# Two weight chunks a step for the quarters, late routing one slot sooner, one-hots ahead of a split, matmuls on zeros at the start, last product in tile order

## The chip, the cores and the metric

The kernel runs on one core of a Trainium2 chip. The metric is the device time of one execution, in microseconds, from all inputs in HBM to all outputs in HBM. The engines are named as in the profile: PE (TensorE), PEld (its weight loads), DVE (VectorE), ACT (ScalarE), POOL (GpSimd) and SP (SyncE, which here issues DMAs).

## What is computed

Three layers in a row, all in fp32: sigmoid attention, a mixture of eight experts with one expert for each token, and a dense layer with a squared ReLU. Cut to what matters (q and k are drawn 4.906 times larger than the 0.1 of the first line):

```
B, H, S, D = 4, 12, 448, 64          # q, k, v: randn * 0.1
scores = q @ k.T / sqrt(D) - log(S)
attn = 1 / (1 + exp(-scores)) @ v    # 1792 tokens x 768
# experts: w_gate (768, 8), w1 (8, 768, 1024), w2 (8, 1024, 768)
logits = x @ w_gate; e = argmax(logits)
gate = exp(logits - max)[e] / (sum(exp(logits - max)) + 1e-9)
x = gate * (relu(x @ w1[e]) @ w2[e])
# dense: w_in (768, 2048), w_out (2048, 768)
h = relu(x @ w_in)
out = (h * h) @ w_out
```

## The kernel before

**Precision.** A product that has to be as exact as fp32 is made of three products of a faster type (fp32r): each operand is split into a high part (ACT copies it into fp32r) and a low part (DVE subtracts), and PE forms high by high, low by high and high by low. The split of a weight chunk (128 x 1536) is `split_w`: wh by ACT (L473), wl by DVE (L474).

**Attention (5.8 to about 180 us).** 24 units, each a pair of heads of one batch. `score` writes score tiles to two PSUM banks (L372, L374), ACT takes the sigmoid (L376), `av` multiplies by v (L382, L385). Unit 0 uses plain fp32 scores, straight from the loaded q and k; the later units use the split form. PE has nothing to do before the first load has come. Finished units are transposed (xn, L421 to L423) and written to x_d in HBM; gate logits come from xT, and `token_logits` copies them into lg (L415). `head` (L190 to L196) makes the one-hots of the experts and their running sum cum. Its first call covers the first three batches, so that the largest expert's tokens can begin early; its second call, at the end of the attention, covers the fourth.

**Expert slots (about 180 to 504 us).** The tokens are sorted by expert into slots of 128; 15 slots are always run, s = 0 to 14. Each has eight steps, c = 0 to 7, one weight chunk each: four of `up` (products ph, L680 to L682), four of `down` (py). Behind each half of `up` ACT takes the ReLU (hr, L722), PE transposes it (L705), ACT and DVE split it (hh L706, hl L707). Behind each step `next_chunk` splits the chunk for the next slot and SP issues the load for the slot behind that. In c = 5 the next slot's rows are transposed, in c = 6 and 7 `fin` copies y out of PSUM (L739) and writes it.

**Routing.** Slots 0 and 1 (FS = 2) hold the early expert. In slot 0 `opening` counts the tokens of all experts on PE (`counts`, L200 to L202, from cum and the one-hots), computes the slots and places on DVE (`slots`, L244 to L257; `late_places`; `spots`, which fills A, L212). In slot 1, c = 0, `pick_rows` turns these into row numbers, by which POOL gathers. In slot 1, c = 6, `late_routing` computes the later slots' rows and gates: 18 small DVE instructions (L815 to L833), one exponential on ACT, three products on POOL (Bg, L837), and SP loads three row starts into registers.

**Quarters.** Up to four remainders of at most 32 rows, NQ = 4, run beside slots 3 to 12. Every two steps there is one event of ten: e = 0 transposes the 32 rows into PSUM tile qa and ACT copies them to qxT; e = 1 to 4 multiply by one `up` chunk each (L785, four matmuls side by side in column groups of 32); e = 5 transposes the hidden rows; e = 6 to 9 take the `down` chunks (L805), and the last copies the result to yq on ACT and writes it. A chunk (128 x 1536) is loaded by `q_load` three chunks ahead (QB = 3 buffers).

**Dense layer (504 to 953 us).** For each of two blocks (4 and 3 token tiles on either half): first layer (pp, L1031 to L1033), then seven products (pq, L1134 to L1136) that make up a Strassen-like scheme; `evac` adds them up on DVE (ob, L1095), and `scatter` (L1001, POOL) writes rows to the output by token number. The last block's last product ends the kernel: its three scatters are issued behind everything else.

**What sets the order.** The order of the program text is the order on each engine; buffers and semaphores do the rest. `order.close()` ends that ahead of the last three scatters.

Of the kernel before, what the change touches and what calls it, by code (L numbers as in the profile page):

```python
# [10 lines left out]
F32 = mybir.dt.float32  # L11
# [11 lines left out]
DM = H * D  # L23
E = 8
# [21 lines left out]
QB = 3  # L46
CH = 1536
# [17 lines left out]
def moe_kernel(ctx: ExitStack, tc: tile.TileContext, qk, v, wg, wm, w2, out):  # L65
# [87 lines left out]
    lg = rt([CP, NR, E], "lg")  # L153
# [3 lines left out]
    eq, z, ez = (rt([CP, NR, E], n) for n in ("eq", "z", "ez"))  # L157
    posA, t30 = rt([CP, E, NR], "posA"), rt([128, E], "t30")
    posi, sli = (rt([CP, NR], n, I32) for n in ("posi", "sli"))
    plf = rt([CP, NR], "plf")  # L160
    A, Bs, Bt = rt([CP, NR, 128], "A", F16), rt([CP, NR, LC], "Bs", F16), rt([CP, NR, LC], "Bt", F16)
# [162 lines left out]
    with ExitStack() as actx:  # L324
# [107 lines left out]

        prev = None
# [129 lines left out]
        token_logits()  # L563
        split_first(2)
        head(FR, NR)
# [89 lines left out]
    with ExitStack() as mctx:  # L655
        w2p = mctx.enter_context(tc.tile_pool(name="w2p", bufs=1, side="right", reuse_waits="tile"))
        mp = mctx.enter_context(tc.tile_pool(name="mp", bufs=2, reuse_waits="tile"))
        ps_x = mctx.enter_context(tc.tile_pool(name="ps_x", bufs=1, space=PS, reuse_waits="tile"))
        ps_h = mctx.enter_context(tc.tile_pool(name="ps_h", bufs=1, space=PS, reuse_waits="tile"))
# [96 lines left out]
        def q_load(n):  # L756
# [5 lines left out]
            qr[n] = mp.tile([128, CH], F32, tag="qraw", name=f"qraw{n}", bufs=QB)  # L762
# [3 lines left out]

        def q_event(k):
            q, e = divmod(k, 10)
            if e == 0:
                qt[0] = ps_q.tile([128, 512], F32, tag="q", name=f"qa_{q}")  # L770
                for j in range(KD):
                    nc.tensor.transpose(qt[0][:, QM * j:QM * j + QM], qx[q][:QM, j * 128:(j + 1) * 128], ident[:QM, :QM])
                qt[1] = mp.tile([128, 256], F32, tag="qT", name=f"qxT_{q}", bufs=1)[:, :KD * QM].rearrange("p (a b) -> p a b", a=KD)
                nc.scalar.activation(qt[1].rearrange("p a b -> p (a b)"), qt[0][:, :KD * QM], AF.Copy)
                if q + 1 < NQ:
                    q_gather(q + 1)
            elif e < 5:
                n = 8 * q + e - 1
                c = QORD[n % 8]
                w = qr.pop(n)  # L780
                o = KD * QM + (c // 2) * 128
                for i in range(3):
                    kk = 3 * (c % 2) + i
                    for j in range(4):
# [6 lines left out]
            elif e == 5:  # L791
                qt[0] = ps_q.tile([128, 512], F32, tag="q", name=f"qb_{q}")
                qt[3] = mp.tile([128, 256], F32, tag="qT", name=f"qhT_{q}", bufs=1).rearrange("p (a b) -> p a b", a=2)
                for i in range(2):
                    nc.tensor.transpose(qt[0][:, i * 128:i * 128 + 128], qt[2][:, i, :], ident)
# [407 lines left out]
```

## Time and profile before

| | us |
|---|---|
| median of 3 runs (lowest, highest) | 963.2 (962.22, 964.21) |
| the profiled execution | 963.18 |
| its span, first to last instruction | 961.7 |
| PE busy | 935.9 (97% of the span) |
| DVE busy | 631.2 (66%) |
| ACT busy | 551.4 (57%) |
| POOL busy | 78.8 (8%) |
| mean granted clock of PE | 0.993 |

How to read it: the span has no long holes on PE. A saving on another engine counts only where PE waits for that engine at that moment; a saving on PE counts everywhere but in a stretch whose end another engine sets. The profile shows one execution; its times are microseconds from the start of the span.

### The profile page before, as it was taken

What the parts mean: (1) busy time and instruction counts of PE and PEld (TensorE: products, weight loads), DVE (VectorE), ACT (ScalarE), POOL (GpSimd) and SP (SyncE); (2) the same over time, 40 slices, a digit from 0 to 9 for tenths busy, and PEclk for the clock granted to TensorE, in tenths of its full rate; (3) what the DMA queues carried; (4) which work ended last, traced back from release to release, by engine and by line L of the source; (5) the groups of instructions that cost most, each with busy time, mean ns of one, the idle gap of its engine ahead of it and who ended that gap; (6) DMA issues with size and microseconds to landing.
All of it is one profiled execution on the core that took longest, in us unless ns stands there. A gap on an engine that the chain in (4) does not pass through costs nothing. (4 is left out here: it accounts for less than half of the span.)

```text
span 961.7 us, 15015 instructions
## 1 busy us (share of the span) xinstructions
PE 935.9 (97%) x5869; PEld 784.7 (82%) x5869; DVE 631.2 (66%) x706; ACT 551.4 (57%) x667; POOL 78.8 (8%) x106
## 2 busy tenths in 40 slices
PE   7999999898999999999998999999999999999996
PEld 3555555487888888888987888889999999999996
DVE  2788866589877776777865676747857521228762
ACT  5767665557777767767753454454534444446550
POOL 1000001024311010100000000010000210000002
PEclk9999999999999999999999999999999999999998
DMA  8798967481487869694447455363244532223312
GB/s 290 255 368 300 357 217 267 164 312 38 170 283 300 326 242 368 225 397 148 162 174 261 183 196 231 132 247 101 97 132 148 169 112 66 66 66 114 117 33 98
DMA packets 52512, 190.63 MB, mean 198 GB/s; under 512 B 8082, under 2 KB 18962, under 8 KB 50386
## 3 DMA queue, kind: packets, MB, share of 16 engines
q1 hardware_dynamic: 34290, 152.77, 45.1%
q0 software_dynamic: 6928, 31.08, 8.4%
q10 hardware_dynamic: 11216, 5.75, 2.1%
q8 instruction: 48, 0.79, 0.3%
q14 instruction: 30, 0.25, 0.1%
HBM read 203.33 MB, written 36.98 MB: 250 GB/s over the span
## 5 line engine op out<-in xcount | busy, mean ns | idle before, releaser
L474 DVE TENSOR_TENSOR wl<-raw,wh 128x1536 fp32r<-128x1536 f32 x110 | 192.6, 1761 | 63.8 <-ACT wh L473 62.0
L473 ACT ACTIVATE wh<-raw 128x1536 fp32r<-128x1536 f32 x110 | 162.9, 1483 | 2.7 <-PE ph L682 0.6
L376 ACT ACTIVATE a<-sc,bias_s 128x896 f32<-128x896 f32 x96 | 82.6, 910 | 56.1 <-PE sc L372 56.0
L1037 ACT ACTIVATE r<-pp 128x512 f32<-128x512 f32 (+1 forms) x64 | 34.8, 544 | 107.4 <-PE pp L1033 107.4
L1134 PE MATMUL pq<-wrh,sh 128*128 128x384 f32 x264 | 89.0, 337 | 0.3 <-DVE ob L1095 0.3
L1135 PE MATMUL pq<-wrl,sh 128*128 128x384 f32 x264 | 88.6, 336 | 0.0
L1136 PE MATMUL pq<-wrh,sl 128*128 128x384 f32 x264 | 88.6, 336 | 0.0
L680 PE MATMUL py<-wh,hh 128*128 128x384 f32 x240 | 84.6, 353 | 0.0
L682 PE MATMUL py<-wh,hl 128*128 128x384 f32 x240 | 81.0, 338 | 2.7 <-DVE hl L707 2.7
L681 PE MATMUL py<-wl,hh 128*128 128x384 f32 x240 | 80.8, 337 | 0.0
L680 PE MATMUL ph<-wh,xh 128*128 128x512 f32 x180 | 75.7, 421 | 1.6 <-ACT xn L422 1.6
L474 DVE TENSOR_TENSOR wrl<-raw,wrh 128x1536 fp32r<-128x1536 f32 x30 | 52.6, 1757 | 36.0 <-ACT wrh L473 36.0
L473 ACT ACTIVATE wrh<-raw 128x1536 fp32r<-128x1536 f32 x30 | 44.4, 1482 | 48.0 <-PE pq L1136 43.1
L682 PE MATMUL ph<-wh,xl 128*128 128x512 f32 x180 | 71.6, 398 | 0.0
L681 PE MATMUL ph<-wl,xh 128*128 128x512 f32 x180 | 71.6, 398 | 0.0
L1045 DVE TENSOR_TENSOR h<-h,h 128x512 f32<-128x512 f32 (+1 forms) x16 | 10.0, 624 | 85.9 <-ACT h L1040 85.9
L1058 DVE TENSOR_TENSOR sl<-h,sh 128x1024 fp32r<-128x1024 f32 (+1 forms) x56 | 59.8, 1085 | 8.7 <-ACT sh L1057 8.6
L382 PE MATMUL po<-a,qkv 128*64 128x448 f32 x288 | 59.6, 548 | 0.0
L1057 ACT ACTIVATE sh<-h 128x1024 fp32r<-128x1024 f32 (+1 forms) x56 | 51.5, 943 | 13.5 <-PE pq L1135 8.0
L1134 PEld LDWEIGHTS pq<-wrh,sh 128*128 128x128 f32 x264 | 49.6, 188 | 0.6 <-issue 0.6
L1135 PEld LDWEIGHTS pq<-wrl,sh 128*128 128x128 f32 x264 | 49.6, 188 | 0.0
L1136 PEld LDWEIGHTS pq<-wrh,sl 128*128 128x128 f32 x264 | 49.6, 188 | 0.0
(289 smaller groups left out, 2088.5 us busy)
## 6 DMA issues: line engine op xcount, KB each, us to landing
raw<-in_wm SPq DMA_DIRECT2D x110, 768.0 KB
qraw<-in_wm SPq DMA_DIRECT2D x32, 768.0 KB
raw<-t_d SPq DMA_DIRECT2D x28, 768.0 KB
cs<-in_w SPq DMA_DIRECT2D x9, 1536.0 KB
raw<-w_d SPq DMA_DIRECT2D x16, 768.0 KB
qkv<-in_qk SPq DMA_DIRECT2D x23, 480.0 KB
whc<-in_w SPq DMA_DIRECT2D x7, 1536.0 KB
t_d<-wlc POOLq DMA_DIRECT2D x7, 1536.0 KB, 7.6
```

Of the source, the lines that this page charges most:

```text
L376: nc.scalar.activation(a[:, :n], ps[:, :n, :S], AF.Sigmoid, bias=bias_s, scale=1.0 / math.sqrt(D))
L382: nc.tensor.matmul(po[64 * h:64 * h + 64, :S], vr[:, 128 * c + 64 * h:128 * c + 64 * h + 64], a[:, h], start=(c == 0), stop=False, skip_gr ...
L473: nc.scalar.activation(h, src, AF.Copy)
L474: nc.vector.tensor_tensor(l, src, f32(h), op=ALU.subtract)
L680: nc.tensor.matmul(ps, lh, rh, start=first, stop=False)
L681: nc.tensor.matmul(ps, lh, rl, start=False, stop=False)
L682: nc.tensor.matmul(ps, ll, rh, start=False, stop=last)
L1057: nc.scalar.activation(sh[:, :2 * N], src, AF.Copy)
L1058: V.tensor_tensor(sl[:, :2 * N], src, f32(sh[:, :2 * N]), op=ALU.subtract)
L1134: nc.tensor.matmul(po[p][:, :DH], lh, wc[:, w0:w0 + DH], start=(q == 0 and kk == 0 and o in (0, 2, 5)), stop=False, **fl)
L1135: nc.tensor.matmul(po[p][:, :DH], lh, wcl[:, w0:w0 + DH], start=False, stop=False, **fl)
L1136: nc.tensor.matmul(po[p][:, :DH], ll, wc[:, w0:w0 + DH], start=False, stop=(q == 3 and kk == 1), **fl)
```

## The change

1. Ahead of the first scores DVE clears a 128 x 448 tile, and PE multiplies it by itself three times, 400 columns, plain fp32, into a bank that nobody reads.
2. The second call of `head` stands ahead of `split_first(2)`.
3. The pool of ph's banks is opened ahead of the pool of the transposes' banks, so each takes other banks of PSUM.
4. `late_routing` is called in slot 1 at c = 0, behind the row numbers and the gathers, no longer at c = 6.
5. lg, z, ez, posA and A lie in one tile `big`, which later serves as a fourth buffer for quarter chunks (each n with n % 4 == 3); chunks are loaded four ahead (QL = 4).
6. A quarter has five events, one every four steps (c = 2 and c = 6 of slots 3 to 12): two `up` chunks, two `up` chunks, the transposes of the hidden rows, two `down` chunks, two `down` chunks. Behind the last of them come yq and, in the same event, the next quarter's transposes (`q_rows`).
7. The last product of the last block runs with the tile as the outer loop and the four parts as the inner one; both remaining splits stand in front of it.

```
+        rest_t = xp.tile([128, S], F32, name="rest_t")
+        nc.vector.memset(rest_t, 0.0)
+        pw = ps_e.tile([128, 512], F32, tag="lgT", name="pw")
+        for i in range(3):
+            nc.tensor.matmul(pw[:, :400], rest_t[:, :128], rest_t[:, :400], start=True, stop=True, skip_group_check=True)
...
         token_logits()
+        head(FR, NR)
         split_first(2)
-        head(FR, NR)
         split_first(3)
...
+        ps_h = mctx.enter_context(tc.tile_pool(name="ps_h", bufs=1, space=PS, reuse_waits="tile"))
         ps_x = mctx.enter_context(tc.tile_pool(name="ps_x", bufs=1, space=PS, reuse_waits="tile"))
-        ps_h = mctx.enter_context(tc.tile_pool(name="ps_h", bufs=1, space=PS, reuse_waits="tile"))
...
+    big = rq.tile([128, CH], F32, tag="big", name="big")
+    lg, z, ez = (big[:CP, 1024 + 128 * i:1152 + 128 * i].rearrange("p (t e) -> p t e", e=E) for i in range(3))
...
+            if n % 4 == 3:
+                qr[n] = rq.tile([128, CH], F32, tag="big", name=f"qraw{n}")
+            else:
+                qr[n] = mp.tile([128, CH], F32, tag="qraw", name=f"qraw{n}", bufs=QB)
...
         def q_event(k):
+            q, e = divmod(k, 5)
+            if e == 2:
+                q_hidden(q)
+                return
+            for r in ((0, 1), (2, 3), (), (4, 5), (6, 7))[e]:
+                (q_up if e < 2 else q_down)(q, r)
+            if e == 4:
+                q_out(q)
                 if q + 1 < NQ:
+                    q_rows(q + 1)
...
+        q_due = {8 * (FS + 1) + 2 + 4 * k: k for k in range(5 * NQ)}
...
                         xg[k] = gather(k)
+                    late_routing()
...
-                if s == 1 and c == 6:
-                    late_routing()
...
+            if lastb and o == len(PRODS) - 1:
+                split_s(4 * o + 2)
+                split_s(4 * o + 3)
+                for p in range(P):
+                    for q in range(4):
+                        product(o, q, p, used[0] + q // 2)
+                break
```

`q_up`, `q_hidden`, `q_down`, `q_rows` and `q_out` are the bodies of the old events, and `product` is the body of the old loop over the tiles.

At three places the order on an engine is shown. DVE at the end of the attention, before (lg: the gate logits; ohz and cum: the one-hots and their running sum; wl: the low part of a weight chunk):

```order
L415 COPY lg<-lgT_1677 112x32
L474 TENSOR_TENSOR wl_1772<-raw_1466,wh_1771 128x1536
L190 TENSOR_REDUCE m<-lg 112x4
L191 TENSOR_TENSOR eq<-lg,m 112x32
L192 TENSOR_TENSOR z<-lg,m 112x32
L193 TENSOR_TENSOR eq<-eq,rev 112x32
L194 TENSOR_REDUCE me<-eq 112x4
L195 TENSOR_TENSOR ohz<-eq,me 112x4x8
L196 SCALAR_TENSOR_TENSOR cum<-seg,ohz 112x136
L474 TENSOR_TENSOR wl_1772<-raw_1466,wh_1771 128x1536
```

The same place on DVE now (lg and z lie in big):

```order
L418 COPY big<-lgT_1679 112x32
L193 TENSOR_REDUCE m<-big 112x4
L194 TENSOR_TENSOR eq<-big,m 112x32
L195 TENSOR_TENSOR big<-big,m 112x32
L196 TENSOR_TENSOR eq<-eq,rev 112x32
L197 TENSOR_REDUCE me<-eq 112x4
L198 TENSOR_TENSOR ohz<-eq,me 112x4x8
L199 SCALAR_TENSOR_TENSOR cum<-seg,ohz 112x136
L482 TENSOR_TENSOR wl_1774<-raw_1468,wh_1773 128x1536 x2
```

The seven instructions of the one-hots moved from between the two splits to ahead of both.

DVE at the start of slot 1, before (idx, tok: the row numbers picked; hl: the low part of the hidden tile):

```order
L273 CAST idx<-r_1872 128x24
L274 TENSOR_SCALAR tok<-r_1872 128x24
L474 TENSOR_TENSOR wl_1473<-raw_1466,wh_1471 128x1536
L474 TENSOR_TENSOR wl_1474<-raw_1466,wh_1472 128x1536
L707 TENSOR_TENSOR hl_2095<-pht_0_2153,hh_2094 128x512
```

And now, the end of the same stretch (the late routing's first 11 instructions stand ahead of these, behind idx and tok):

```order
L852 TENSOR_TENSOR r_128<-r_128,srowT 128x20
L853 CAST gp<-gr 112x16
L854 TENSOR_SCALAR beyond<-r_128,sx 128x20
L855 TENSOR_TENSOR r_128<-r_128,beyond 128x20
L856 TENSOR_SCALAR ctl<-r_128 128x20
L857 TENSOR_TENSOR gr<-gr,gp 112x16
L858 CAST gp<-gr 112x16
L482 TENSOR_TENSOR wl_1475<-raw_1468,wh_1473 128x1536
L482 TENSOR_TENSOR wl_1476<-raw_1468,wh_1474 128x1536
L715 TENSOR_TENSOR hl_2097<-pht_0_2205,hh_2096 128x512
```

The late routing now stands between the row numbers and the first two splits of slot 1.

PE in slot 5 at c = 2, the end of the first quarter, before (qb: the quarter's result):

```order
L705 MATMUL pht_0_3115<-ident,hr_0_3103 128x128 x4
L680 MATMUL ph_1_3108<-wh_1771,xh_2955 128x512
L681 MATMUL ph_1_3108<-wl_1772,xh_2955 128x512
L682 MATMUL ph_1_3108<-wh_1771,xl_2956 128x512
L805 MATMUL qb_2880<-qraw_2938,qhT_2881 32x96 x16
L680 MATMUL ph_1_3108<-wh_1771,xh_2955 128x512
```

And now (qa: the next quarter's transposes):

```order
L713 MATMUL pht_0_3101<-ident,hr_0_3089 128x128 x4
L688 MATMUL ph_1_3094<-wh_1773,xh_2941 128x512
L689 MATMUL ph_1_3094<-wl_1774,xh_2941 128x512
L690 MATMUL ph_1_3094<-wh_1773,xl_2942 128x512
L817 MATMUL qb_2884<-qraw_2769,qhT_2885 32x96 x16
L817 MATMUL qb_2884<-qraw_2785,qhT_2885 32x96 x16
L781 MATMUL qa_3156<-ident,qx_2610 128x32 x6
L688 MATMUL ph_1_3094<-wh_1773,xh_2941 128x512
```

The last two chunks stand in a row, and the next quarter's transposes, which stood two steps later, stand right behind them; they write the bank that yq is copied from.

## Rows read from the trace of the kernel before

**Rows 1.** Waits of PE: line, waited for, us in total, times, longest.

```profile
PE r L200 <- DVE cum L196: 2.9, 1, 2.9
PE py L682 <- DVE hl L707: 2.7, 1, 2.7
PE ph L680 <- ACT xn L422: 1.6, 1, 1.6
```

**Rows 2.** Timeline of the opening: start, length, engine, line, [idle before <- releaser].

```profile
5.84 4.51 PE L372 MATMUL sc<-qkv 64*128 64x448 f32 x12 [5.84 <-DMA qkv<-in_qk]
...
11.46 0.47 PE L372 MATMUL sc<-qkh 64*128 64x448 f32 x2
...
12.87 2.48 PE L382 MATMUL po<-a,qkv 128*64 128x448 f32 x12
...
9.25 2.75 ACT L376 ACTIVATE a<-sc,bias_s 128x896 f32<-128x896 f32 x3 [0.46 <-PE sc L372]
```

**Rows 3.** Windows: us, PE busy, other engines, granted clock, DMA share, GB/s.

```profile
5.84:10.35 4.51, 4.51 (x13) 1.74 (x13) 2.58 (x4) 2.01 (x2) 0.00 (x0) 1.00 1.04 392
...
187.49:190.91 3.42, 3.42 (x11) 0.52 0.01 2
...
236.25:254.00 17.75, 17.75 (x123) 1.00 0.59 195
```

**Rows 4.** Timeline of slot 0, DVE and ACT.

```profile
183.88 1.76 DVE L474 TENSOR_TENSOR wl<-raw,wh 128x1536 fp32r<-128x1536 f32 x1 [3.23 <-ACT wh L473]
...
186.77 0.44 DVE L196 TENSOR_TENSOR_SCAN cum<-seg,ohz 112x136 bf16<-112x136 bf16 x1
...
191.33 0.60 ACT L722 ACTIVATE hr<-ph 128x512 f32<-128x512 f32 x1 [0.24 <-PE ph L682]
...
195.27 0.68 DVE L707 TENSOR_TENSOR hl<-pht,hh 128x512 fp32r<-128x512 f32 x1
```

**Rows 5.** Timeline of slot 1 and the start of slot 2, DVE.

```profile
209.16 1.76 DVE L474 TENSOR_TENSOR wl<-raw,wh 128x1536 fp32r<-128x1536 f32 x1 [0.84 <-ACT wh L473]
212.30 1.76 DVE L474 TENSOR_TENSOR wl<-raw,wh 128x1536 fp32r<-128x1536 f32 x1 [1.39 <-ACT wh L473]
...
226.00 0.16 DVE L815 TENSOR_TENSOR sa<-sa 128x8 f32<-128x8 f32 x1
...
229.85 5.74 DVE L474 TENSOR_TENSOR wl<-raw,wh 128x1536 fp32r<-128x1536 f32 x3
```

**Rows 6.** Timeline of POOL, the late routing's products.

```profile
227.38 0.84 POOL L837 TENSOR_TENSOR Bg<-Bs,gp 112x384 bf16<-112x384 f16 x1 [15.63 <-DVE gp L824]
...
230.00 2.31 POOL L837 TENSOR_TENSOR Bg<-Bs,gp 112x384 bf16<-112x384 f16 x1 [0.62 <-DVE gp L833]
```

**Rows 7.** Timeline of a quarter's event on PE, and one wh on ACT.

```profile
253.32 0.39 PE L682 MATMUL ph<-wh,xl 128*128 128x512 f32 x1
253.64 0.86 PE L785 MATMUL qa<-qraw,qxT 128*32 128x128 f32 x24
254.43 0.50 PE L680 MATMUL ph<-wh,xh 128*128 128x512 f32 x1
254.77 0.40 PE L681 MATMUL ph<-wl,xh 128*128 128x512 f32 x1
255.00 0.40 PE L682 MATMUL ph<-wh,xl 128*128 128x512 f32 x1
...
265.76 1.48 ACT L473 ACTIVATE wh<-raw 128x1536 fp32r<-128x1536 f32 x1
```

**Rows 8.** Groups of the page: line engine op, count, busy, mean ns, idle before.

```profile
L1058 DVE TENSOR_TENSOR sl<-h,sh 128x1024 fp32r<-128x1024 f32 (+1 forms) x56 | 59.8, 1085 | 8.7 <-ACT sh L1057 8.6
```

**Rows 9.** Timeline of the end, DVE and POOL.

```profile
952.26 0.97 POOL L1001 DMA_INDIRECT out<-ob,idx  x1 [3.66 <-DVE ob L1095]
...
953.02 0.56 DVE L1095 TENSOR_TENSOR ob<-pq,ob 128x384 f32<-128x384 f32 x1 [0.49 <-PE pq L1136]
...
954.82 0.97 POOL L1001 DMA_INDIRECT out<-ob,idx  x1 [0.30 <-issue]
```

More of the change, by code (lines that the diff above doesn't have):

```diff
@@ new lines, in q_rows @@
+        def q_rows(q):
+            qt[0] = ps_q.tile([128, 512], F32, tag="q", name=f"qa_{q}")
+            for j in range(KD):
+                nc.tensor.transpose(qt[0][:, QM * j:QM * j + QM], qx[q][:QM, j * 128:(j + 1) * 128], ident[:QM, :QM])
+            qt[1] = mp.tile([128, 256], F32, tag="qT", name=f"qxT_{q}", bufs=1)[:, :KD * QM].rearrange("p (a b) -> p a b", a=KD)
+            nc.scalar.activation(qt[1].rearrange("p a b -> p (a b)"), qt[0][:, :KD * QM], AF.Copy)
+            if q + 1 < NQ:
+                q_gather(q + 1)
@@ new lines, in q_up @@
+        def q_up(q, r):
+            n = 8 * q + r
+            c = QORD[n % 8]
+            w = qr.pop(n)
+            o = KD * QM + (c // 2) * 128
+            for i in range(3):
+                kk = 3 * (c % 2) + i
+                for j in range(4):
+                    nc.tensor.matmul(qt[0][QM * j:QM * j + QM, o:o + 128], qt[1][:, kk, :], w[:, i * 512 + 128 * j:i * 512 + 128 * j + 128],
+                                     start=(kk == 0), stop=(kk == KD - 1), skip_group_check=True, tile_position=(0, QM * j))
+            if r == 3:
+                qt[2] = mp.tile([128, 256], F32, tag="qh", name=f"qh_{q}", bufs=1).rearrange("p (a b) -> p a b", a=2)
+                nc.scalar.activation(qt[2].rearrange("p a b -> p (a b)"), qt[0][:, KD * QM:KD * QM + 256], AF.Relu)
+            q_load(n + QL)
@@ new lines, in q_hidden, with q_down @@
+        def q_hidden(q):
+            qt[0] = ps_q.tile([128, 512], F32, tag="q", name=f"qb_{q}")
+            qt[3] = mp.tile([128, 256], F32, tag="qT", name=f"qhT_{q}", bufs=1).rearrange("p (a b) -> p a b", a=2)
+            for i in range(2):
+                nc.tensor.transpose(qt[0][:, i * 128:i * 128 + 128], qt[2][:, i, :], ident)
+            nc.scalar.activation(qt[3].rearrange("p a b -> p (a b)"), qt[0][:, :256], AF.Copy)
+        def q_down(q, r):
+            n = 8 * q + r
+            c = QORD[n % 8]
+            fg, dh = (c - 4) // 2, c % 2
+            w = qr.pop(n)
+            o = 256 + 96 * dh
+            for f in range(4):
+                for j in range(4):
+                    nc.tensor.matmul(qt[0][QM * j:QM * j + QM, o:o + 96], qt[3][:, fg, QM * f:QM * f + QM], w[:, f * 384 + 96 * j:f * 384 + 96 * j + 96],
+                                     start=(fg == 0 and f == 0), stop=(fg == 1 and f == 3), skip_group_check=True, tile_position=(0, QM * j))
+            q_load(n + QL)
@@ L943, in moe_kernel @@
                     nc.gpsimd.dma_start(out=yq_d[:, :, DM:DM + 1].rearrange("q t a -> t q a"), in_=tok[:QM, NSLOT:].bitcast(F32).unsqueeze(2))
[L944 removed]
+                    for n in range(QL):
                         q_load(n)
@@ L1127, in moe_kernel @@
                 for p in range(P):
[L1128 to L1138 removed]
+                    product(o, q, p, used[0])
+                sp.pop(g)
                 adds(o, q)
```

97 lines of the change are left out of this document (29 added, 68 removed).

## Prediction

> **What bounds the kernel now.** I began with the page: PE is busy for 935.9 of the 961.7 us of the span, so time is to be won where PE waits, where it runs at half clock, or where its records show overhead beside streaming. Next came the list of what PE waited for [rows 1]. Its largest entry, the first load, is not touched; three others lie where the change acts: 2.9 us for the running sum of the one-hots, 2.7 for the low half of a hidden tile, 1.6 for a copy out of the bank that the first MoE product takes. Together 7.2 us. Then I read four stretches in order of time: the opening [rows 2], slot 0 [rows 3, 4], slots 1 and 2 [rows 5, 6], one event of a quarter [rows 7], and at the end the last product [rows 8, 9]. The profiled run took 963.18 us and its span 961.7, so 1.5 us lie around the span; the median of the three runs is 963.2, the same within 0.02. I subtract every gain from 963.18. A difference of 0.2% (1.93 us) is about what a measurement of this kernel can tell from none.
>
> **Opening matmuls on zeros: gain 1.2 us.** The six plain fp32 score matmuls of unit 0 (12 records) take 4.51 us from 5.84; six fp32 matmuls of the same columns, paired in the same way, take 2.48 at 12.87 [rows 2]. The first ones ran at about half rate, 1.2 GHz instead of 2.4, after an engine that had done nothing. Yet the granted clock of 5.84 to 10.35 reads 1.00 [rows 3]; the record and the durations disagree, and I go by the durations. If the zeros lift the clock in time, a score tile takes 2.48/3 = 0.83, the first is there at 6.67, and then ScalarE's sigmoids are the limit, because there are two score banks: three at about 2.75/3 = 0.92 make 2.75, so the next unit's scores start at about 9.4, with the way from engine to engine about 9.8, instead of at 11.46 [rows 2]. That is 1.66 at the most. Nothing is the other end, and below that the zeros could run into the load's arrival and delay PE by a few tenths (−0.3). I take 1.2, since the clock may rise only within the first tile. PE has no other wait until slot 0 in the list [rows 1], so a shift there arrives.
>
> **Slot 0: gain 1.2 us.** The swap of the pools takes ph out of the bank that xn is copied from, and the 1.6 us wait goes; the one-hots ahead of the split take the 2.9 us wait [rows 1]. These sums don't add up, because VectorE's chain sets the end of slot 0. Before its split at 183.88 VectorE is idle for 3.23 us; then the one-hots end at 186.77 + 0.44 = 187.21, and all that follows runs almost back to back to hl at 195.27 to 195.95, which PE's first down product takes [rows 4]. The split begins at 183.88 in any case (it waits for ScalarE), the one-hots, 187.21 − (183.88 + 1.76) = 1.57 us of work, fit into the idle 3.23, and the chain behind them comes 1.57 sooner. This is the upper end. PE finishes sooner than that, so its wait moves on to hr at 191.33 and the hl behind it [rows 4]: if the clock falls in that wait as it did to 0.52 behind the present one (187.49 to 190.91 [rows 3]), 3.42 × 0.48 = 1.6 us are lost, as they are now, and the end is still VectorE's. Lower end: nothing, if the first pass over the hidden tile waits for ScalarE's own split. I take 1.2.
>
> **Late routing a slot sooner: gain 1.1 us.** Now its 18 small VectorE instructions run from 226.00 to 229.85, 3.85 us, and the three splits behind it take 5.74 [rows 5]; at their end the hidden tile's low half is late by 2.73 (2.7 in [rows 1]), and this wait goes. In slot 1 the same 3.85 us are put behind the picked rows, ahead of the splits at 209.16 and 212.30. VectorE is idle there for 0.84 and 1.39, 2.23 together [rows 5]. What doesn't fit, 3.85 − 2.23 = 1.62, makes hl, next behind the splits, late, and PE waits for it: 2.73 − 1.62 = 1.1. Bounds: 2.0, if the routing's own gaps close up; −0.8, if only part of the idle time can be used (3.5 us of stall). ScalarE's one exponential and the three products on GpSimd move along. So do SyncE's three register loads: they wait for the row starts, and the weight loads of that step are queued behind them, which are needed a slot later.
>
> The third product on GpSimd began at 230.00, under a split, and took 2.31, against 0.84 for one that didn't [rows 6]: GpSimd waited, not VectorE. The Trainium skill ("SBUF — State Buffer", section "SBUF: two separate sides") says that a VectorE operation with two SBUF inputs and a GpSimd operation that reads SBUF exclude each other, whichever begins first, for a whole instruction. By that rule the splits of slot 1 can be held up as well, by three products of 0.84, about 2.5 at the worst; part of it would still be idle time, and the time would come out near 957.4. I keep to the row, in which the split went first.
>
> **Quarters: gain 2.8 us.** At a chunk's event [rows 7] PE starts 0.09 late (253.32 + 0.23 = 253.55, start 253.64), the 24 records take 254.43 − 253.64 = 0.79 until the next matmul, and that one lasts 0.34 (to 254.77) where its follower lasts 0.23 (to 255.00): 0.20 of switching beside the body. Two chunks in a row save this once: 0.20 for each of 16 pairs, 3.2. The body may hold such a share too: its 12 fp32 matmuls (two records each) run four side by side, so three times 128 columns stream, and at 0.83 us for 448 columns [rows 2] that is 0.71 of the 0.79. I take this 0.08 along: 0.28 × 16 = 4.5. The next quarter's six transposes behind the last pair save about 0.2 at three places, 0.57. Against this: they write the bank from which yq is still to be copied, so they wait for ScalarE, and there yq stands behind wh of the same step, 1.48 us [rows 7], which can only begin when PE has ended that chunk's matmuls. A pair lasts 2 × 0.79 = 1.58, so wh is covered and the copy itself is not: below the 0.60 that the larger hr copy takes [rows 4], 0.58 with the way. At the one place of the three where the step also has a y copy ahead of wh, another 0.5 by the same row: 0.58 + 1.1 + 0.58 = 2.26. Sum 4.5 + 0.57 − 2.26 = 2.8. Ends: 0.4 (0.20 a pair, the waits half as long again) and 4.0 (the waits half as long).
>
> The Trainium skill ("TensorEngine Tiling (Array Packing)", section "Key Properties") says that a change of the tiling mode drains TensorE. The 0.09 ahead of the group agrees. By this rule the transposes behind a pair are one more change, and keeping them there saves about 0.3 less over the three places; the time would be 956.7.
>
> **Last product tile by tile: gain 0.5 us.** The three last scatters go one behind the other from 952.26, and the last starts at 954.82, though its sum on VectorE is over at 953.02 + 0.56 = 953.58 [rows 9]. With the tiles in turn the first two scatters are long gone, and the last one starts when its sum is there: at most 1.24 sooner. Other end: the two splits now stand together in front, and the first tile reaches the fourth part sooner; a split is 1.085 us on VectorE [rows 8], so −1.1 if the second is late by a whole one. I take 0.5.
>
> The packing of scratch into one tile costs nothing: the same instructions on other addresses, and the fourth buffer's first load waits for the last use of that scratch in slot 2, before the point where the loads are issued.
>
> **Sum.** 1.2 + 1.2 + 1.1 + 2.8 + 0.5 = 6.8; 963.18 − 6.8 = 956.4. All best ends together, 1.66 + 1.57 + 2.0 + 4.0 + 1.24 = 10.5, would give 952.7.
>
> **Rivals.**
> *A: ScalarE takes the quarters' gain.* If yq and the copies of the next quarter stand behind more of ScalarE's work than I counted, the pairs save 0.20 each and the waits at three places double (4.5): 3.2 + 0.57 − 4.5 = −0.7 in place of 2.8, time about 959.9. For it: at every one of these places wh waits for PE itself. Against: only three places.
> *B: the routing falls on slot 1 in full*, 3.5 us of stall against 2.73 removed (−0.8 in place of 1.1), and slot 0 gains nothing because its end waits for ScalarE: 956.4 + 1.9 + 1.2 = 959.5; with a half-clock stretch like that at 187.49 [rows 3], 1.6 more, 961.1. For it: VectorE's idle time in slot 1 is itself a wait for ScalarE's splits.
> *C: the zeros don't do what they are there for.* The granted clock at the start already reads 1.00 [rows 3], and then nothing is to be lifted: 956.4 + 1.2 = 957.6.
> *D, the other side: the second chunk of a pair is late.* Now a chunk is used every two steps; then two at once, and both come through one queue between the reloads. A chunk of 128 x 1536 fp32 numbers, 786 KB, at the 195 GB/s of 236.25 to 254.00 [rows 3] takes about 4.0 us. If at six of the pairs (two for each quarter at its start, whose loads have only eight steps' lead, three quarters) half a transfer is missing, PE waits 6 × 2.0 = 12: 968.4. It is slower than before as soon as the 16 pairs wait 6.8/16 = 0.43 us each in mean. Against: the list has no wait for a chunk of a quarter at all [rows 1], the DMA share there is 0.59 [rows 3], and a fourth buffer is added.
>
> **How the numbers follow.** Forecast 0.54, A 0.17, B 0.13, C 0.10, D 0.06. The range of 8 in 10 takes the forecast with its bounds, A, C and most of B: 952.7 to 961.0. Faster by over 0.2% is below 961.25: the forecast, C, A and B but for the part in which they coincide (some 0.09), 0.84. Within 0.2%: that part, 0.09. Slower: D and a little, 0.07.
>
> **What would show it.** Opening: the 12 records of unit 0 take about 2.5 to 3.5 us, and the next scores start near 10. Slot 0: neither the wait for cum nor that for xn is in the list; a wait for hr's transposes or for hl, at a PE end 1.2 to 1.6 us sooner, is. Slots 1 and 2: no wait for hl in slot 2, one of 1.3 to 1.7 in slot 1; B is right if it is above 2.7. Quarters: 16 pairs that each cost about 1.7 beside the matmuls around them (now 2 × 0.99: 254.77 − 253.55 less 0.23), and three waits of 0.5 to 1.2 ahead of the transposes; A is right if they come to over 4. Tail: the last scatter starts under 1 us behind the last sum. The prediction is wrong if a wait for qraw stands in the list, or if half clock spreads over the slots that now run at 1.00.

## The result and the profile after

The changed kernel takes 951.92 us (median of 4 runs, 950.93 to 953.03) against 963.71 (4 runs, 962.22 to 964.72): a ratio of 0.9879, 95% interval 0.9862 to 0.9897. It is 11.8 us faster; 6.8 were forecast, and the time lies below the range. Both kernels were profiled twice (963.18 and 964.24 us before, 953.03 and 951.19 after). Cut at the same instructions of TensorE, the two pairs show where the time went (us saved; a minus is a loss):

| stretch | forecast | first pair | second pair |
|---|---|---|---|
| opening, to the first product by v | 1.2 | 0.33 | 1.49 |
| attention's end and slot 0 | 1.2 | 2.63 | 3.21 |
| slots 1 and 2 | 1.1 | −1.24 | 0.25 |
| slots 3 to 14 (quarters) | 2.8 | 3.78 | 3.71 |
| start of the dense layer to its first pq | 0 | 4.38 | 4.04 |
| the rest of the dense layer | 0 | −0.19 | −0.12 |
| from the last product's final records to the end | 0.5 | 0.46 | 0.47 |
| sum | 6.8 | 10.15 | 13.05 |

The largest row is one that the forecast does not have. First the list of TensorE's waits in the kernel after (line, waited for, us, times, longest), to be laid beside [rows 1]:

```profile
PE py L690 <- DVE hl L715: 2.4, 1, 2.4
PE qa L781 <- ACT yq L823: 2.0, 3, 0.9
PE pht L713 <- ACT hr L730: 2.0, 1, 2.0
PE pw L440 <- DVE rest_t L437: 1.7, 1, 1.7
PE pp L1056 <- ACTq L986: 0.7, 1, 0.7
PE sc L375 <- ACT a L379: 0.5, 2, 0.4
```

All three waits of [rows 1] are gone, and waits of much the same length for hl and hr have come, the first a slot earlier than before. Seen from this list alone little was won. What else is gone is a wait that [rows 1] left out, because nothing in the change touches its place. In the list of the kernel before it stands between the 2.7 and the 1.6:

```profile
PE pp L1032 <- issue: 2.6, 1, 2.6
```

Timeline of the kernel before, behind the jump over the extra slots (the slots beyond the 15, which a branch at L961 skips; in the kernel after it is at L986):

```profile
504.36 0.47 PE L1031 MATMUL pp<-yt,wrh 128*128 128x512 f32 x1 [0.86 <-ACTq L961]
507.44 0.39 PE L1032 MATMUL pp<-yt,wrh 128*128 128x512 f32 x1 [2.61 <-issue]
```

And its window there (us, PE busy and the other engines, granted clock, DMA share, GB/s):

```profile
508.00:512.00 4.00, 4.00 (x12) 3.10 (x11) 3.93 (x3) 0.00 (x0) 0.00 (x0) 0.57 1.01 407
```

TensorE runs one product, waits 2.61 us for nothing that the list names ("issue"), and then has a mean granted clock of 0.57 over 4 us, the 1.2 GHz level for most of them. The same place after:

```profile
498.86 0.50 PE L1056 MATMUL pp<-yt,wrh 128*128 128x512 f32 x1 [0.71 <-ACTq L986]
499.19 0.40 PE L1057 MATMUL pp<-yt,wrh 128*128 128x512 f32 x1
499.43 0.40 PE L1058 MATMUL pp<-yt,wrl 128*128 128x512 f32 x1
```

No wait, and no half clock (1.00 from 498 to 502): 4.38 us.

### The profile page after: what moved, and what is told of

It is laid out like the page before. It is cut to its first block, busy times and chain, and to the rows that moved or that the text cites. A ratio compares the mean times of both kernels' runs of the same rounds, so it can differ in the third digit from the quotient of the medians.

```text
span 951.5 us, 15019 instructions
## 1 busy us (share of the span) xinstructions
PE 933.4 (98%) x5875; PEld 787.7 (83%) x5875; DVE 631.7 (66%) x707; ACT 552.3 (58%) x667; POOL 80.3 (8%) x106
```

## Experiments

Each kernel was timed beside the kernel before; since that kernel's median differs between the chips (962.5 to 964.1), kernels are compared by their ratios to it, and a difference of ratios is turned into us at 963.7. The intervals of the ratios are some ±0.002, ±2 us, so a term of 1 us is read from the traces.

### Moving the jump's target without doing anything else

```diff
+        tiny_t = xp.tile([128, 32], BF16, name="tiny_t")
+        nc.vector.memset(tiny_t, 0.0)
+        pw = ps_e.tile([128, 512], F32, tag="lgT", name="pw")
+        for i in range(8):
+            nc.tensor.matmul(pw[:32, :32], tiny_t, tiny_t, start=True, stop=True, skip_group_check=True)
         prev = None
```

> The kernel before, with eight bf16 matmuls of 32 x 32 on zeros at the very start, where TensorE waits for the first load anyway; nothing else differs. In the trace of before, TensorE runs one product behind the jump over the extra slots (504.36), waits 2.61 us with no releaser named, and then runs at a granted clock of 0.57 until about 511.5; the same stretch lasts 4.38 us less in the changed kernel. Theory P (place of the code): the wait is a fetch of TensorE's instructions, and it is there because the target of the jump lies a few instructions ahead of the end of a fetched block; eight more matmuls ahead of it move the target past that end, so the wait and the half clock go: 4.4 us less, about 959.3, with no 'issue' wait at the dense layer's start. The Trainium skill (Runtime: NRT & Kernel Launch, section Instruction fetch mechanics) says that a taken branch to a target outside the fetched blocks stalls. Rival R (an effect of the change on other engines or queues, or chance of one execution): the wait of 2.6 stays, time within 1 us of before.

Measured: 957.87 us against 963.08, ratio 0.9949 (0.9931 to 0.9967), 5 us less from eight matmuls that compute nothing. In its list of waits there is no "issue" any more, only

```profile
PE pp L1036 <- ACTq L966: 0.7, 1, 0.7
```

and the stretch from the dense layer's start to its first pq lasts 4.43 us less than in the kernel before. Theory P holds, and R falls: none of the seven changes is in this kernel. (It does clear a tile and use a bank more; the kernel with two zeros below has no such difference. Ahead of the dense layer its trace gains 0.9: 2.2 by the end of slot 0, of which 1.6 are lost in slots 1 and 2; both are taken up below.)

### Without the zeros, and with two of them

```diff
-        rest_t = xp.tile([128, S], F32, name="rest_t")
-        nc.vector.memset(rest_t, 0.0)
-        pw = ps_e.tile([128, 512], F32, tag="lgT", name="pw")
-        for i in range(3):
-            nc.tensor.matmul(pw[:, :400], rest_t[:, :128], rest_t[:, :400], start=True, stop=True, skip_group_check=True)
```

```diff
-        for i in range(3):
+        for i in range(2):
             nc.tensor.matmul(pw[:, :400], rest_t[:, :128], rest_t[:, :400], start=True, stop=True, skip_group_check=True)
```

> The changed kernel without the opening matmuls on zeros and their clearing. The opening: the trace of after has the second unit's scores only 0.34 us sooner than before, so I expect 0.3 us lost there (my prediction of 1.2 would mean 1.2). By theory P the three fp32 matmuls are also twelve TensorE instructions ahead of the jump; without them its target lies about five instructions ahead of where it was in before, so that four or so products run behind the jump, and then the wait returns, shorter: 1.5 to 2.2 us, with half clock behind it, 3 to 4 us in all, total 955 to 956. By rival R nothing returns at the dense layer's start, total near 952.3.

> The changed kernel with two instead of three matmuls on zeros (1.7 to 4.6 us instead of 1.7 to 6.1). If the clock has risen by the first scores all the same, these take 2.5 for 12 records and start at the load's arrival. If it falls back or hasn't risen in the gap, the 12 records take about 4.5 again, as without zeros. For theory P this is a third place of the jump's target, four TensorE instructions ahead of the changed kernel's and eight behind that without zeros, which ran four products before it waited 2.20: it lies at the end of a block then, and either there is no wait or one of 2.6 to 3 with no or one product ahead of it.

Measured: 956.47 (ratio 0.9928, 0.9914 to 0.9943) without them, 4.7 more than the changed kernel; 957.18 in one run with two. Timeline of TensorE without the zeros, where the dense layer starts:

```profile
498.96 0.47 PE L1051 MATMUL pp<-yt,wrh 128*128 128x512 f32 x1 [0.87 <-PEq L981]
499.27 0.40 PE L1052 MATMUL pp<-yt,wrh 128*128 128x512 f32 x1
499.50 0.40 PE L1053 MATMUL pp<-yt,wrl 128*128 128x512 f32 x1
499.73 0.40 PE L1051 MATMUL pp<-yt,wrh 128*128 128x512 f32 x1
502.33 0.43 PE L1052 MATMUL pp<-yt,wrh 128*128 128x512 f32 x1 [2.20 <-issue]
```

The same with two zeros:

```profile
501.78 0.40 PE L1056 MATMUL pp<-yt,wrh 128*128 128x512 f32 x1 [3.78 <-issue]
```

This kernel differs from the changed one by a single matmul, so no bank, no tile and no other engine is left as the cause. The instructions of TensorE can serve as a ruler. Each fp32 matmul on zeros is two records and two weight loads, and each product of the dense layer one record and one weight load. Counted in the traces up to the first product (pp), with the place of the wait:

| kernel | instructions ahead | products before the wait | wait | block landed | TensorE goes on |
|---|---|---|---|---|---|
| changed, no zeros | 7002 | 4 | 2.20 | 500.94 | 502.33 |
| before, pools swapped (below) | 7006 | 2 | 2.01 | 504.21 | 505.70 |
| before | 7008 | 1 | 2.61 | 506.06 | 507.44 |
| before, second trace | 7008 | 1 | 2.29 | 507.06 | 508.54 |
| changed, two zeros | 7010 | 0 | 3.78 | 500.34 | 501.78 |
| changed (three zeros) | 7014 | no wait | | 500.41 | |

With two instructions for each product that ran, and the weight load of the next, the wait stands behind instruction 7011 in all five traces that have it (the 3.78 includes the 0.7 to 0.9 that every kernel waits at the jump); the twelve traces without it count 7014 to 7023 ahead of the first product. That there were four products without zeros, and one in the kernel before, is due to six instructions more in the latter, all of them waits for semaphores.

The page of each trace lists TensorE's instructions as a DMA queue of their own: 16 KB a packet, one packet for some 246 of TensorE's 11806 instructions. The kernel before, and then the kernel after:

```profile
q8 instruction: 48, 0.79, 0.3%
```

```profile
q8 instruction: 47, 0.77, 0.3%
```

The five traces with the wait have 48 packets, the twelve others 47. The times of single packets (the column "block landed") show what is waited for. The jump's own record lasts 3.5 to 4.0 us in every trace and ends 1.36 to 1.39 behind the landing of a packet. The Trainium skill ("Runtime: NRT & Kernel Launch", section "Instruction fetch mechanics") says that a taken branch whose target isn't in the window of instructions already fetched waits for a fetch; the traces agree. The next packet starts only 0.7 to 1.5 behind the end of the jump; where nine instructions or fewer are left of the target's block, TensorE runs out of them and goes on 1.38 to 1.49 behind that packet's landing. Where the target lies in the block behind, 12 to 16 products run by that time, and nothing is waited for. So the wait that the list calls "issue" is one for instructions.

The zeros' own effect: opening of the kernel after, the same place in its second trace, and then the opening with two zeros.

```profile
1.73 4.37 PE L440 MATMUL pw<-rest_t 128*128 128x400 f32 x6 [1.73 <-DVE rest_t L437]
6.16 2.46 PE L375 MATMUL sc<-qkv 64*128 64x448 f32 x8
...
11.12 0.48 PE L375 MATMUL sc<-qkh 64*128 64x448 f32 x2 [0.16 <-ACT a L379]
```

```profile
5.90 1.77 PE L375 MATMUL sc<-qkv 64*128 64x448 f32 x8 [0.39 <-DMA qkv<-in_qk]
```

```profile
1.74 3.03 PE L440 MATMUL pw<-rest_t 128*128 128x400 f32 x4 [1.74 <-DVE rest_t L437]
5.76 4.87 PE L375 MATMUL sc<-qkv 64*128 64x448 f32 x12 [0.99 <-DMA qkv<-in_qk]
...
11.73 0.47 PE L375 MATMUL sc<-qkh 64*128 64x448 f32 x2
```

Two matmuls and a pause of 0.99 us leave the scores at half rate (4.87 for 12 records, 4.51 in [rows 2]). Three lift it: behind the first tile in the first trace, without a pause (8 records in 2.46), and from the first record in the second, with a pause of 0.39 (1.77). Whether the third matmul or the shorter pause does it was not separated. Rival C falls, although the granted clock reads 1.00 in all these windows, as in [rows 3]. The first product by v starts at 11.45 to 12.54 in eleven traces with three zeros and at 12.74 to 13.59 in six without or with two: about 1.2 on the mean, as forecast, and the first trace of the kernel after had the latest start of its eleven.

### Late routing: back, and in pieces

```diff
                         xg[k] = gather(k)
-                    late_routing()
...
+                if s == 1 and c == 6:
+                    late_routing()
```

> The changed kernel with late routing back in slot 1 at c = 6. From the two traces slot 1 lost 4.30 us and slot 2 won 3.06 by the move, so putting it back should win 1.2: about 950.7, with a wait of 2.7 for hl in slot 2 and no half clock behind it, and none in slot 1. By the prediction's own term (the move wins 1.1) it loses 1.1: about 953.0.

Measured: 952.52, ratio 0.9883 (0.9865 to 0.9901): 0.4 more than the changed kernel, no difference that can be told. The expectation took slot 2 of the first trace for granted: there the wait of 2.73 for hl is followed by full clock. In this kernel, in the one with small matmuls and in the second trace of the kernel before, the same wait is followed by half clock, and 1.2 to 1.6 us more are lost. Windows of the kernel before, first trace and second:

```profile
237.00:238.00 1.00, 1.00 (x8) 1.00 (x7) 1.00 (x2) 0.00 (x0) 1.00 (x1) 1.00 0.76 160
```

```profile
237.00:238.00 1.00, 1.00 (x5) 1.00 (x4) 1.00 (x2) 0.00 (x0) 1.00 (x1) 0.50 0.63 197
```

So the move neither wins nor loses anything that can be told; it takes a wait from slot 2 to slot 1. Why it didn't win 1.1 is to be seen in slot 1 of the kernel after, on VectorE and on GpSimd:

```profile
207.38 2.15 DVE L855 TENSOR_TENSOR r<-r,beyond 128x20 f32<-128x20 f32 x1
...
209.94 4.07 DVE L482 TENSOR_TENSOR wl<-raw,wh 128x1536 fp32r<-128x1536 f32 x2
213.94 0.68 DVE L715 TENSOR_TENSOR hl<-pht,hh 128x512 fp32r<-128x512 f32 x1
```

```profile
207.84 1.64 POOL L862 TENSOR_TENSOR Bg<-Bs,gp 112x384 bf16<-112x384 f16 x2
210.12 2.28 POOL L862 TENSOR_TENSOR Bg<-Bs,gp 112x384 bf16<-112x384 f16 x1 [0.63 <-DVE gp L858]
```

A VectorE operation of 20 columns takes 2.15 us: it ends when two products on GpSimd (207.84 to 209.48) have ended. The routing takes 4.67 instead of 3.85 [rows 5], and the two splits, with the third product between them, 4.07 instead of 2 × 1.76. TensorE's wait is 2.44, not 1.62, and half clock follows:

```profile
214.67 0.44 PE L690 MATMUL py<-wh,hl 128*128 128x384 f32 x1 [2.44 <-DVE hl L715]
```

```profile
215.50:216.50 1.00, 1.00 (x6) 1.00 (x5) 1.00 (x2) 0.00 (x0) 0.00 (x0) 0.64 0.00 0
216.50:217.50 1.00, 1.00 (x5) 0.91 (x4) 1.00 (x1) 0.00 (x0) 0.00 (x0) 0.50 0.00 0
217.50:218.50 1.00, 1.00 (x6) 1.00 (x5) 0.45 (x1) 0.29 (x1) 0.00 (x0) 0.50 0.00 0
```

The next kernel cuts the routing into five pieces (SyncE's row starts now stand ahead of GpSimd's products, which are the last piece):

```diff
         def late_routing():
...
+            yield
...
+                    late = late_routing()
+                if s == 1 and c in (0, 1, 3):
+                    next(late, None)
...
+                if s == 1 and c in (5, 6):
+                    next(late, None)
```

> The changed kernel with late routing in five pieces: slot 1 at c = 0, 1, 3, 5, and the three products on GpSimd at c = 6. Theory: the routing fits into VectorE's idle time if no piece is longer than that of its step and no product on GpSimd stands against a waiting VectorE operation; then the wait for hl in slot 1 (2.45) and the half clock behind it (about 1.7) go, and none comes in slot 2: 947.8 to 948.5. Rival (VectorE is simply full in slots 1 and 2): the wait moves to another place and at most 1 us is won.

Measured: 948.63, ratio 0.9852 (0.9827 to 0.9878), 2.6 less; in the trace slot 1 lasts 4.20 less than in the kernel after and slot 2 the same. The waits for hl in slots 1 and 2 are gone. VectorE isn't full; the work only has to be cut to the size of its gaps. How much of the gain is due to the smaller pieces, and how much to the products' later place, was not separated.

### Quarters: one chunk an event, and the transposes later

The first kernel has the old plan of ten events with the new helpers and four buffers:

```diff
         def q_event(k):
-            q, e = divmod(k, 5)
...
+            q, e = divmod(k, 10)
+            if e == 0:
+                q_rows(q)
+            elif e < 5:
+                q_up(q, e - 1)
+            elif e == 5:
+                q_hidden(q)
+            else:
+                q_down(q, e - 2)
+                if e == 9:
+                    q_out(q)
...
-        q_due = {8 * (FS + 1) + 2 + 4 * k: k for k in range(5 * NQ)}
+        q_due = {8 * (FS + 1) + 2 * k: k for k in range(10 * NQ)}
```

The second keeps the pairs:

```diff
                 q_out(q)
-                if q + 1 < NQ:
-                    q_rows(q + 1)
...
+            elif n - 2 in q_due and q_due[n - 2] % 5 == 4 and q_due[n - 2] // 5 + 1 < NQ:
+                q_rows(q_due[n - 2] // 5 + 1)
```

> The changed kernel with one quarter chunk an event every two steps, and the next quarter's transposes in an event of their own two steps behind the last chunk; the four buffers stay. From the traces slots 3 to 13 last 3.6 us less in the changed kernel. If that is the pairs (theory of the prediction: 0.28 a pair, less the waits for yq), 2.8 to 3.8 us return: 954.7 to 955.7. If most of it came with the fourth buffer or with other places of PSUM (rival), under 1 us returns.

> The changed kernel with the pairs kept, but the next quarter's transposes two steps behind the last pair instead of right behind it. The three waits for yq (2.0 us in the trace of after) go, and three more switches of about 0.2 come: 1.4 us less, about 950.5. If the waits only hide other waits of ScalarE or GpSimd (the gather of the quarter behind), nothing is won: 952.

Measured: 956.03 (0.9931, 0.9915 to 0.9947) with single chunks, 5.0 more, of which its trace shows 3.5 from slot 3 to slot 14; there each of the slots 3 to 13 lasts as long as in the kernel before, within 0.06. So the gain is the pairs', not the buffer's or the banks'. With the transposes later 949.64 (0.986, 0.9838 to 0.9882), 1.8 less, 1.69 in the slots of its trace: the waits for yq, 2.03, are gone, and three more changes between the two kinds of matmul cost the difference, 0.34. A pair in the kernel after:

```profile
251.59 0.39 PE L690 MATMUL ph<-wh,xl 128*128 128x512 f32 x1
251.91 1.52 PE L795 MATMUL qa<-qraw,qxT 128*32 128x128 f32 x48
253.36 0.50 PE L688 MATMUL ph<-wh,xh 128*128 128x512 f32 x1
253.69 0.40 PE L689 MATMUL ph<-wl,xh 128*128 128x512 f32 x1
```

Counted as in the forecast: from 251.59 + 0.23 to 253.69, less 0.23, is 1.64, against 2 × 0.99 in [rows 7]. A pair saves 0.34, not 0.28: 0.20 of switching as read, and 0.13 of the body (1.45 for two against 2 × 0.79), where 0.08 was worked out.

### Slot 0: one-hots, pools, and a copy on ScalarE

```diff
         token_logits()
-        head(FR, NR)
         split_first(2)
+        head(FR, NR)
```

> The changed kernel with the one-hots back between the two splits. My theory: VectorE's chain sets the end of slot 0, so 1.57 us of one-hots moved out of VectorE's idle time return in full: a wait for cum of about 2.9 comes back, slot 0 lasts 0.9 to 1.6 us longer, 952.8 to 953.5. Rival: ScalarE's split and the wait for hr set the end, and nothing moves (below 0.3).

Measured: 952.92 (0.9893, 0.9874 to 0.9913), 1.3 more by the ratios, inside their intervals; the wait for cum is back with 2.6, half clock follows it, and slot 0 lasts 0.45 longer than in the first trace of the kernel after and 1.15 longer than in the second. In that first trace the wait for hr was followed by half clock too, in the second it wasn't. This fits the theory, with 0.5 to 1.2 us for the one-hots and the clock as the unsteady part.

> The changed kernel with the pools in the old order. In the kernel before with small matmuls at the start, the bank that these took had already moved the others, and ph waited 0.28 for the copy lg instead of 1.6 for xn. Theory S (the swap isn't needed once the opening's bank is there): a wait of about 0.3 ahead of the first ph, end of slot 0 unchanged, 952 plus or minus 0.5. Rival: the 1.6 us wait for xn returns and shifts all behind it: 953.6.

> The kernel before with the two pools of banks in the new order, nothing else. The prediction's reading: the wait of 1.6 for xn goes, but VectorE's chain sets the end of slot 0, and xn and the splits behind it on ScalarE stay where they are, so nothing is won: 963, within 0.6. Theory X: the wait of 1.6 isn't due to the bank but to the transfer that xn waits for, and it goes or stays by chance; time likewise 963, and where xn is on time, slot 0 begins 1.3 to 1.7 sooner. Rival: the swap by itself wins 1.7.

In the changed kernel back, in the kernel before forward:

```diff
-        ps_h = mctx.enter_context(tc.tile_pool(name="ps_h", bufs=1, space=PS, reuse_waits="tile"))
         ps_x = mctx.enter_context(tc.tile_pool(name="ps_x", bufs=1, space=PS, reuse_waits="tile"))
+        ps_h = mctx.enter_context(tc.tile_pool(name="ps_h", bufs=1, space=PS, reuse_waits="tile"))
```

Measured: 951.51 (0.9876, 0.9855 to 0.9898), nothing lost; and 961.78 against 962.46 (0.9994, 0.9984 to 1.0004), nothing won that can be told. But, counted from the first product by v, the trace of the swap alone has slot 0 begin 1.70 sooner, and so has every trace but the two of the kernel before, whatever its pools (1.3 where ph first waits for the copy lg: the kernel with small matmuls and the changed kernel with the pools back). ScalarE in the first trace of the kernel before, and then in the kernel with the pools swapped:

```profile
177.35 0.60 ACT L422 ACTIVATE xn<-pt 112x512 f32<-112x512 f32 x1 [1.64 <-PE pt L421]
177.98 0.31 ACTq L423 DMA_DIRECT2D x_d<-xn  x1
181.38 0.60 ACT L422 ACTIVATE xn<-pt 112x512 f32<-112x512 f32 x1 [3.43 <-DMA x_d<-xn]
```

```profile
178.12 0.60 ACT L422 ACTIVATE xn<-pt 112x512 f32<-112x512 f32 x1 [1.64 <-PE pt L421]
178.75 0.31 ACTq L423 DMA_DIRECT2D x_d<-xn  x1
180.14 0.60 ACT L422 ACTIVATE xn<-pt 112x512 f32<-112x512 f32 x1 [1.42 <-PE pt L421]
```

In the kernel before the last xn waits for an earlier xn's way to HBM (3.39 in the second trace), and everything behind it on ScalarE, both splits among it, comes 2 us later. Why this transfer ends so late in just these two traces, and whether it does so in all runs of that kernel, stays open: the swap's timed runs say hardly, since 1.7 would show in them. It matters for the table's second row: the kernels with small matmuls and with the pools swapped have the one-hots in their old place, and their traces reach the end of slot 0 sooner by 2.2 and 2.0 all the same.

The last kernel here stands on the two edits that won (late routing in pieces, transposes later), with ScalarE's copy sa moved:

```diff
-        nc.scalar.activation(sa[:, 2, 1:], pn, AF.Copy)
...
             elif c == 4:
+                nc.scalar.activation(sa[:, 2, 1:], pn2, AF.Copy)
                 late_places(prk2)
```

> Both edits that won by themselves: late routing in five pieces, and the next quarter's transposes two steps behind the last pair. If they are independent, their gains against the changed kernel add up, 3.3 + 2.3 = 5.6: about 946.3. If they use the same idle time of ScalarE or VectorE, less: 947.5 to 948.6.

> As the kernel with both edits, and ScalarE's small copy sa, which in slot 0 waits 1.44 us for VectorE while wh and hr stand behind it, goes to c = 4. Theory: hr comes 1.4 sooner, the wait of 2.0 for hr becomes about 0.6, then the wait for hl (0.6 where the clock held) sets the end: 0.5 to 0.8 less where the clock held, up to 1.6 less where it fell behind the wait; about 945.3. Rival: VectorE's hl at 191.7 to 192.4 is the end already: 946.3, no change.

Measured: 946.21 (0.9818, 0.9804 to 0.9832) with both edits, 5.9 less than the changed kernel; the two gains add up (4.20 and 1.69 in their traces; 2.6 and 1.8 by their ratios, the same within the intervals), and no kernel tried is faster. With the copy moved 946.32 (0.9819, 0.9806 to 0.9833): no change. Its waits tell why:

```profile
PE py L689 <- DVE hl L714: 2.2, 1, 2.2
...
PE pht L712 <- ACT hr L729: 0.4, 1, 0.4
```

The wait for hr went from 2.0 to 0.4, the wait for hl came from 0.6 to 2.2. VectorE's chain is the end of slot 0, as the forecast had it.

### Last product in the old order

```diff
-            if lastb and o == len(PRODS) - 1:
+            if False and lastb and o == len(PRODS) - 1:
```

> The changed kernel with the last product in the old order (parts outside, tiles inside, splits two parts ahead). Prediction's term: the new order wins 0.5 (at most 1.24), so about 952.4 and the last scatter 1.2 behind the last sum. Rival: the new order wins nothing, since the last transfer to HBM and not the issue of the scatters ends the kernel: 951.9, within 0.2.

Measured: 953.03 (0.9885, 0.987 to 0.9901), 0.6 more, inside the intervals. In the trace of the old order the last sum and the last scatter are

```profile
942.79 0.56 DVE L1120 TENSOR_TENSOR ob<-pq,ob 128x384 f32<-128x384 f32 x1 [0.49 <-PE pq L1151]
```

```profile
944.59 0.97 POOL L1026 DMA_INDIRECT out<-ob,idx  x1 [0.30 <-issue]
```

and in the new one

```profile
943.33 0.56 DVE L1120 TENSOR_TENSOR ob<-pq,ob 128x384 f32<-128x384 f32 x1 [3.61 <-PE pq L1151]
```

```profile
944.66 0.97 POOL L1026 DMA_INDIRECT out<-ob,idx  x1 [0.60 <-issue]
```

944.59 − (942.79 + 0.56) = 1.24 behind the sum against 944.66 − (943.33 + 0.56) = 0.77: the 0.5 of the forecast.

### Second traces of both kernels

> The kernel before, unchanged, for a second trace. Place of the code (P): the wait of 2.6 behind the first product of the dense layer is there again, with half clock behind it. Theory X (the last xn waits for an earlier xn's transfer by the chance of one execution): the wait of 1.6 ahead of the first ph is gone and slot 0 begins 1.3 to 1.7 sooner; rival: it is there again, since ph's bank or the order of transfers makes it. The wait for hl of 2.7 in slot 2 is there; whether half clock follows it is open (none in the first trace, 1.2 to 1.6 us lost in two other kernels).

> The changed kernel, unchanged, for a second trace. No 'issue' wait at the dense layer's start (P). The second unit's scores start anywhere from 10.0 to 11.1, by when the loads land, since seven traces with three matmuls on zeros lie in that range. Waits as in the first trace: hr 2.0, hl 2.4 in slot 1, yq 2.0 in three places.

Measured: 964.24 and 951.19 in one run each. The kernel before has its wait behind the jump again (2.29), the wait for xn again (1.6), and this time half clock in slot 2. The kernel after has the waits of its first trace, no wait behind the jump, and full clock behind the wait for hr. The start of the first product by v, 11.61, lies in the range of the others.

## Why the prediction failed, point by point

- **What bounds the kernel now: this step failed.** It took, of the list of waits, only those "where the change acts", and so left out the 2.6 us without a releaser and the half clock behind it; the sum had no term for 4.0 to 4.4 us of the 11.8. No timing of work explains them: with the change TensorE has 7014 instead of 7008 instructions ahead of the first product behind the jump, and the jump's target came to lie in the next block of instructions. The kernels with small matmuls, and with none, two and three zeros, show it to the instruction.
- **Opening:** mechanism and size right, about 1.2 on the mean of the traces; the two pairs show 0.3 and 1.5. The delay of 0.3 that stood as the worst end occurred in the first: the zeros ended at 6.1, and the scores began at 6.16 for 5.84.
- **Slot 0:** mis-sized, 2.6 to 3.2 for 1.2. VectorE's chain is the limit, as said. The sentence that failed is "The split begins at 183.88 in any case": ScalarE's wh stood behind the late xn, and that went too, which is worth 2.0 to 2.2 in the kernels that keep the one-hots where they were. The one-hots' own part is 0.5 to 1.2, as forecast. How much of the 2.0 belongs to most runs of the kernel before is open. That the wait moves on to hr (2.0) and that half clock may follow it was right.
- **Late routing:** wrong in size, and in the first pair in sign, −1.2 and 0.3 for +1.1. The stall was 2.44 us, not 1.62, because VectorE was held up by GpSimd's products, and half clock followed, another 1.9 and 1.7 in slot 1 of the two traces. "GpSimd waited, not VectorE" was wrong already for the kernel before: the three splits of [rows 5] took 5.74, not 3 × 1.76 = 5.28, and two small operations of the routing took 0.79 and 0.77 (after the change 0.17 for the like of the first). Each began 0.1 behind a product, that at 227.38 [rows 6] and the one shown here, and ended 0.03 behind that product's end:

```profile
228.54 0.84 POOL L837 TENSOR_TENSOR Bg<-Bs,gp 112x384 bf16<-112x384 f16 x1 [0.32 <-DVE gp L828]
227.46 0.79 DVE L826 TENSOR_TENSOR gr<-g,gp 112x16 f32<-112x16 f32 x1
228.64 0.77 DVE L830 TENSOR_TENSOR r<-r,beyond 128x20 f32<-128x20 f32 x1
```

  The rule of the Trainium skill ("SBUF — State Buffer", section "SBUF: two separate sides") that stood there against the change was the better guide: VectorE waits for whole products of GpSimd, and GpSimd for whole splits. These rows of the kernel before agree with its order, too, that the first to begin holds the other up. The 2.15 us do not, by the records: that operation began at 207.38, 0.46 ahead of the first product, and still waited for two. Spans of GpSimd are rough in the profile, so this stays open. Rival B had its place right (slot 1) with a price too high for the wait (3.5) and too low for the clock (1.6).
- **Quarters:** right in mechanism, mis-sized by 0.9: a pair saves 0.34, not 0.28, and the three waits for yq cost 0.54, 0.95 and 0.54, 2.03 for 2.26. Rival A falls. The transposes behind a pair save 0.34 at the three places, not 0.57, near the 0.3 less that the next paragraph of the prediction allowed for; 16 × 0.34 + 0.34 − 2.03 = 3.75 is what the slots show (3.78 and 3.71). That they bring less than they cost was not seen, though both prices stood in the text: 0.57 against 2.26.
- **Tail:** 0.5, as forecast. **Rival D:** no wait for qraw is in the list.

Without the row of the jump the first pair of traces has 5.8 and the second 9.0, around the 6.8 of the sum. That is luck: late routing came out 2.3 and 0.9 below its term, slot 0 1.4 and 2.0 above, the quarters 1.0 and 0.9 above.

## To carry to other kernels

List every wait of the engine that sets the time, also those with no releaser and in places that a change doesn't touch, and ask of a wait right behind a jump whether it hangs on where the code lies; a few empty instructions ahead of the jump test that in one run, and the packets of the instruction queue show the fetch. Put long strings of small instructions into the gaps of a busy engine in pieces no longer than the gap, and look at what GpSimd does in that moment. An operation that takes several times its usual time beside a neighbour's is the row to look for.

## What was not expected of the hardware

- The jump of TensorE lasts 3.5 to 4.0 us here, of which its matmuls wait for 0.7 to 0.9, and a second wait comes behind it when nine instructions or fewer are left of its target's 16 KB block: 2.20, 2.01, 2.61 or 2.29, and 3.78 us with nine, five, three and one left; none in the traces whose target lies in the next block. Half clock comes behind the wait, 1.5 to 1.8 us more.
- The same wait of TensorE at the same place is followed by the 1.2 GHz level in one execution and not in the next: 2.73 for hl in slot 2 (1.00 and 0.50 in the two traces of the kernel before), 2.0 for hr in slot 0 (0.50 in one trace of the kernel after, full in the other). Between the two traces this makes 1.4 us in that slot 2 and 0.7 in that slot 0.
- The granted clock reads 1.00 in the opening, where score products take about twice their later time (4.51 for 12 records, 2.48 for twelve of the same columns later). The record and the durations were not reconciled.
